# More banks for spare matmuls, and VectorE work moved between groups, in a fused two-attention kernel

## Chip, cores and metric

The kernel runs on one NeuronCore of a Trainium2 chip. The metric is the device time of one execution in microseconds (us), as a median of separate runs. TensorE does the matmuls (PE in the profile, its weight loads are PEld), ScalarE (ACT) does the exponentials, VectorE (DVE) the elementwise work, SyncE (SP) issues most transfers.

## What is computed

Two attention layers read the same input of 2,048 rows and 640 columns, with 32 heads of 20 columns each. Layer A is full softmax attention; layer B looks at eight earlier positions, two apart. A gate per row mixes the two.

```
def _A_ref(x, wqkv, wo):
    ...
    scores = jnp.einsum("bhqd,bhkd->bhqk", q, k) * scale
    p = _softmax(scores, axis=-1)
    o = jnp.einsum("bhqk,bhkd->bhqd", p, v)
    return (...)(o, 0, 2, 1, 3).reshape(B, S, D) @ wo
...
def _B_ref(x, wqkv, wo):
    W, dil = 8, 2
    ...
    logits = jnp.einsum("bhsd,bhswd->bhsw", q, kg) * scale
    logits = jnp.where(mask[None, None, :, :], logits, -1e9)
    attn = _softmax(logits, axis=-1)
    o = jnp.einsum("bhsw,bhswd->bhsd", attn, vg)
    return (...)(o, 0, 2, 1, 3).reshape(B, S, D) @ wo
...
g = _sigmoid((x * gate_w).sum(-1, keepdims=True))
return g * a + (1 - g) * b
```

## The kernel before

**Groups and units.** Layer A is worked in 32 groups: four chunks of 512 queries, and in each chunk eight quads of four heads. A group has 64 units, one for each of 16 key blocks and four heads. A unit is the score matmul of 128 keys against 512 queries (L1172, it fills one PSUM bank), an exponential and a value matmul (L1196). PSUM has eight banks. Banks 0 to 2 and 3 to 4 take the scores in turn: a step of the kernel is one exponential of ScalarE over three banks, the next over two (`mk_exp`, L1187). The value matmuls of a group add up in bank 5 (`OB`), each head in its own strip of 32 partitions. At the end of a group VectorE transposes bank 5 out (`do_norm`, L644), and only then can the next group's values start there.

**Units on VectorE.** `XN` gives for each of the 32 groups how many of its units are not exponentiated on ScalarE. `gen_x` (L985 to L1020) does such a unit: a score matmul (L995) into a side bank, seven VectorE operations that make the exponential by a polynomial (L1000 to L1008), and a value matmul into bank 5 (L1017). The tuple adds up to 36 units, which leaves 2,012 units and 805 steps for ScalarE.

**Lanes.** Banks 6 and 7 are side banks. All other work is written as generators, called lanes, that take a side bank, fill it by matmuls, let VectorE copy it out, and give it back: `gen_k`, `gen_q` and `gen_v` make layer A's keys, queries and values; `gen_F` projects layer B's queries and keys and its logits (L827, L843); `gen_K` projects layer B's values, does its softmax (L900 is its exponential on ScalarE) and the weighted sum over eight positions on VectorE (L957, L961); `gen_fold` applies the output weights and sends the result out (L694); `gen_prefold` does so for the last chunk up to its last two quads. `FWIN`, `KWIN` and `OWIN` give, for each chunk, the groups between which the lanes F, K and O (fold) are paced: before the first number the lane isn't due, by the second it should be done, and from the step before that on it is due at every step. A lane also waits for what it depends on, for example K of chunk 1 for K of chunk 0.

**The planner.** The order of every engine's instructions is made when the program is built. A loop over the 805 steps (L1351) books costs on a clock for each engine (`clk`), issues the score matmuls two steps ahead, holds values back until three steps are pending or bank 5 is free (`flush`, L1408), then lets due lanes issue what fits before TensorE's and VectorE's limits for this step (`lim_pe`, `lim_dve`). `take` (L438) marks a side bank as held and `give` (L455) frees it, with the time at which its last copy ends in `free_at`. Waits follow from what tasks read and write (`task`, L82). A task that *writes* a buffer waits for the last writer and for all readers, also when the last writer is on its own engine. A task that *accumulates* waits for readers, but not for an earlier writer on its own engine.

**Spare matmuls.** After the lanes, the loop at L1492 adds matmuls whose result nobody reads. It aims at so much side work on TensorE for each step that is pending:

```
while pair_side < FILL * min(3, npend) and clk["pe"] + MM + SWITCH <= lim_pe and s < NS - 2 and npv[0] == 0:
    if not idle_mm():
        break
```

`FILL` is two matmuls of 512 columns, `MM` is booked as 0.216 us. `idle_mm` (L1303) writes a side bank that no lane holds (L1315, identity times a piece of the input). If there is none, it accumulates zeros onto bank 5 (L1319), if that bank is neither read nor still to be read by VectorE. Otherwise it does nothing. Where spares are still missing after an even step, the next score matmuls are issued twice or three times (`dup`).

Of the kernel before, what the change touches and what calls it, by code (L numbers as in the profile page):

```python
# [13 lines left out]
P = 128  # L14
# [4 lines left out]
CN = D // P  # L19
# [13 lines left out]
XMIN = -126.0 / (SCALE * 1.4426950408889634)  # L33
XLOG = float(np.log(2.0 / XC4))

XN = (1, 2, 0, 2, 0, 2, 1, 2, 0, 0, 0, 0, 0, 1, 2, 1, 1, 0, 0, 3, 0, 2, 1, 1, 2, 2, 3, 1, 1, 1, 2, 2)
FWIN = ((3.5, 2.1), (8.7, 7.6), (13.9, 21.4), (20.8, 24.3))
KWIN = ((7.6, 8.5), (9.5, 12.4), (12.6, 24.7), (24.0, 23.4))
OWIN = ((6.1, 13.1), (13.7, 23.5), (15.7, 31.2))
XPOS = ((7, 1), (9, 2), (5, 0), (11, 3))  # L40


# [203 lines left out]
def _build(ctx, nc, A_x, A_wqkv, A_wo, B_wqkv, B_wo, gate_w, out):  # L246
# [83 lines left out]
    def fap(t, first, dims):  # L330
        return bass.AP(tensor=t, offset=first.offset, ap=[[first.ap[0][0], P]] + dims)
# [97 lines left out]

    held = {6: False, 7: False}  # L430
    free_at = {6: 0.0, 7: 0.0}
    forcing = [0]
    cur = [None]
    EAGER = "kqvx"
# [3 lines left out]
    def take():  # L438
        while True:
            free = [b for b in (6, 7) if not held[b]]  # L440
            me = cur[0].name if cur[0] is not None else ""
            hot = me[:1] in EAGER
            if hot:
                wanting.add(me)
            if free and (hot and (me[0] != "v" or not any(w[0] != "v" for w in wanting)) or not wanting or forcing[0]):
                b = min(free, key=lambda k: free_at[k])
                if forcing[0] or free_at[b] <= clk["pe"] + 100.0:
                    held[b] = True
                    wanting.discard(me)
                    if cur[0] is not None:  # L450
                        cur[0].hold += 1
                    return b
            yield ("poll",)
# [12 lines left out]
    def chain(b, mms, reads, w=1.0, cost=MM):  # L466
        n = len(mms)
        for k, m in enumerate(mms):
            yield ("pe", cost, w)
            t = mm_part(b, [m], k, n, reads, cost)  # L470
        return t

# [4 lines left out]
    def v_chunk(b, p, gi, kb, i_):  # L477
        lo, hi = VG[gi]
        w0, wn = (1, 161) if p == 0 else (2 + 160 * p, 160)

        def fn(e):
            ins = None
            for c in range(CN):
                ins = e.matmul(bank[b][:, i_ * wn:(i_ + 1) * wn], xT[:, c, kb * P:(kb + 1) * P],  # L484
                               WvA[:, c, w0:w0 + wn], start=(c == 0), stop=(c == CN - 1))
            return ins

        rd = ["xT"] + (["WvA0", "WvA1"] if p == 0 else ["WvA"])
        if i_ == 0:
            return T("pe", fn, reads=rd, writes=[("bk", b)], cost=375)  # L490
        return T("pe", fn, reads=rd, accum=[("bk", b)], cost=375)
# [303 lines left out]
    def gen_F(tc):  # L795

        while not latedone[0] or (tc > 0 and not fdone.get(tc - 1)):
            yield ("poll",)
        xk = [("x_tm", t) for t in range(NCH)] if tc == 0 else []
        if tc == 0:  # L800
            T("dve", lambda e: e.memset(kB[:, :, 0:PADB], 0.0), writes=["kB"] + xk, cost=100)
        else:
            T("dve", lambda e: e.tensor_copy(kB[:, :, 0:PADB], kB[:, :, 512:512 + PADB]), reads=["kB"], writes=["kB"], cost=170)
        for kind in ("q", "k"):
            for f in range(CN):
                b = yield from take()
                w0 = f * P if kind == "q" else D + f * P
                mms = [(bank[b], WqkB[:, c, w0:w0 + P], xT[:, c, tc * 512:(tc + 1) * 512]) for c in range(CN)]
                t = yield from chain(b, mms, ["WqkB", "xT"])
                dst, key = (qB[:, f, :], "qB") if kind == "q" else (kB[:, f, PADB:PADB + 512], "kB")  # L810
                yield ("dw", t.fin, 690.0, 0.0)
                give(b, T("dve", lambda e, dst=dst, b=b: e.tensor_copy(dst, bank[b]), reads=[("bk", b)], writes=[key], cost=690))  # L812
        while tc > 0 and not ldone.get(tc - 1):
            yield ("poll",)
        while (NQUAD - 1) not in wk_made:
            yield ("poll",)
        for half in range(2):
            b = yield from take()
            slot = {}

            def sel(f, b=b, slot=slot):
                rs = [slot[(f, wp)] for wp in range(4)]

                def pe_l(e):
                    ins = None
                    for wp in range(4):
                        ins = e.matmul(bank[b][32 * wp:32 * wp + 32, :], Sel[:, f, :], prod[rs[wp]][:, :],  # L827
                                       start=(f == 0), stop=(f == CN - 1))
                    return ins

                rd = [("prod", r) for r in rs] + ["Sel"]
                if f == 0:
                    return T("pe", pe_l, reads=rd, writes=[("bk", b)], cost=340)
                return T("pe", pe_l, reads=rd, accum=[("bk", b)], cost=340)

            for idx in range(4 * CN):
                f, wp = divmod(idx, 4)
                r = prodctr[0] % NPR
                prodctr[0] += 1
                slot[(f, wp)] = r  # L840
                off = PADB - DIL * (4 * half + wp)
                yield ("dve", 416.0, 0.2)
                t = T("dve", lambda e, r=r, f=f, off=off: e.tensor_tensor(prod[r][:, :], qB[:, f, :], kB[:, f, off:off + 512],  # L843
                                                                      ALU.mult),
                      reads=["qB", "kB"], writes=[("prod", r)], cost=416)
                if idx >= 5 and idx % 4 == 1:
                    yield ("pe", 340.0, 0.0)
                    sel(idx // 4 - 1)
            yield after(t)
            yield ("pe", 340.0, 0.0)  # L850
            t = sel(CN - 1)
            yield ("dw", t.fin, 690.0, 0.0)
            give(b, T("dve", lambda e, half=half, b=b: e.tensor_copy(lgt[half], bank[b]),
                      reads=[("bk", b)], writes=[("lgt", half), ("WkA", 1)], cost=690))
        if tc == 0:
            for w in range(1, WIN):
                row = 32 * (w % 4)
                T("dve", lambda e, w=w, row=row: e.memset(lgt[w // 4][row:row + 32, 0:DIL * w], -1.0e9),
                  writes=[("lgt", w // 4)], cost=60)
        fdone[tc] = True  # L860

    def gen_K(tc):
# [25 lines left out]
            return ins  # L888

        yield ("pe", 550.0, 300.0)  # L890
        t = T("pe", pe_tf, reads=[("lgt", 0), ("lgt", 1), "ident"], writes=[("bk", b)], cost=550)
        yield ("dw", t.fin, 690.0, 690.0)
        give(b, T("dve", lambda e, b=b: e.tensor_copy(L_flat, bank_bf[b]), reads=[("bk", b)], writes=["L"], cost=690))
# [43 lines left out]
        yield after(mk_rep(0))  # L937
        b = yield from take()
        yield ("pe", 550.0, 300.0)
        t = mk_aT(0, b)  # L940
        yield ("dw", t.fin, 690.0, 690.0)
        give(b, ev_aT(0, b))
        for bl in range(4):
            ai = bl % 2
            for w in range(WIN):
# [23 lines left out]
                if w == 3 and bl < 3:  # L969
                    yield after(tr)  # L970
                    b = yield from take()
                    yield ("pe", 550.0, 300.0)
                    tm = mk_aT(bl + 1, b)
                if w == 4 and bl < 3:
                    yield ("dw", tm.fin, 690.0, 690.0)
# [9 lines left out]
    def gen_x(gi, k, u):  # L985
# [3 lines left out]
        while gi > 0 and not (gi in ql and ql[gi].done):  # L989
# [2 lines left out]
        kA, kB_, kC = "xA", "xB", "xC"  # L992
        b = yield from take()
        yield ("pe", MM, 0.0)
        t = T("pe", lambda e: e.matmul(bank[b], kT[32 * j:32 * j + 32, q, kb * P:(kb + 1) * P], qT[gi % NQT][32 * j:32 * j + 32, :],  # L995
                                       start=True, stop=True),
              reads=[("kT", q, kb // 4), ("qT", gi % NQT)], writes=[("bk", b)], cost=MM)
# [304 lines left out]

    def idle_mm():  # L1303

        free = [b for b in (6, 7) if not held[b] and free_at[b] <= clk["pe"] + 50.0]
        obs = [sch.bufs[("ob", j)] for j in range(4)]
        if not free and (any(o[1] for o in obs) or any(o[0].stream != "pe" for o in obs)):
            return False
        sw = 0.0 if block[0] else SWITCH
        clk["pe"] += sw  # L1310
        block[0] = True
        block[1] += MM
        if free:
            b = free[0]
            T("pe", lambda e: e.matmul(bank[b], ident[:, :], xT[:, 0, 0:512], start=True, stop=True),  # L1315
              reads=["xT", "ident"], writes=[("bk", b)], cost=MM)
        else:

            T("pe", lambda e: e.matmul(bank[OB], zt[:, :], fap(ident, ident[:, 0:1], [[0, 4], [1, P]]), start=False, stop=False,  # L1319
                                       skip_group_check=True),  # L1320
              reads=["zt", "ident"], accum=[("ob", j) for j in range(4)], cost=MM)
        return True

    kl, vl, ql, foldl, xl = {}, {}, {}, {}, {}
# [221 lines left out]
```

## Time and profile before

| | |
|---|---|
| three timed runs | 950.94, 953.43, 954.73 us; median 953.43 |
| the profiled execution, its own time | 949.74 us |
| its span, first to last instruction | 947.9 us |
| mean granted TensorE clock | 0.995 |
| ScalarE busy | 927.7 us, 831 instructions |
| VectorE busy | 702.7 us, 1,305 instructions |
| TensorE busy by its modelled ends | 846.1 us, 6,241 matmuls |
| exponentials of three banks (402) and two (403) | 1,579 and 1,152 ns each |
| spare matmuls, by weight loads | 251 of L1315, 31 of L1319 |

A row of the profile that begins with a line number is a group of like instructions: line, engine, operation, output and inputs, count, busy time in us and mean of one in ns, and the idle time before them with what ended it. An exponential's own time is longer than the distance to the next one, since ScalarE starts an instruction before the last has left it; the distance between starts is what counts. A stretch is a piece of the span with each engine's busy time in it and the TensorE clock that was granted, 1.00 at full speed.

### The profile page before, as it was taken

What the parts mean: (1) busy time and instruction counts of PE and PEld (TensorE: products, weight loads), DVE (VectorE), ACT (ScalarE), POOL (GpSimd) and SP (SyncE); (2) the same over time, 40 slices, a digit from 0 to 9 for tenths busy, and PEclk for the clock granted to TensorE, in tenths of its full rate; (3) what the DMA queues carried; (4) which work ended last, traced back from release to release, by engine and by line L of the source; (5) the groups of instructions that cost most, each with busy time, mean ns of one, the idle gap of its engine ahead of it and who ended that gap; (6) DMA issues with size and microseconds to landing.
All of it is one profiled execution on the core that took longest, in us unless ns stands there. A gap on an engine that the chain in (4) does not pass through costs nothing.

```text
span 947.9 us, 16453 instructions
## 1 busy us (share of the span) xinstructions
PE 846.1 (89%) x6241; PEld 284.9 (30%) x6337; DVE 702.7 (74%) x1305; ACT 927.7 (98%) x831; POOL 3.1 (0%) x7
## 2 busy tenths in 40 slices
PE   8989899988888888999888899888888999889897
PEld 5333233322222222333222223322222233322232
DVE  5687664756777888548989775788898867898853
ACT  5999999999999999999999999999999999999997
POOL 1000000000000000000000000000000000000000
PEclk9999999999999999999999999999999999999999
DMA  9000000000000000000000000000000000000000
GB/s 312 9 1 4 22 13 1 1 22 16 1 1 2 1 1 1 8 8 8 8 1 1 1 1 8 8 9 1 8 2 1 1 8 8 15 1 1 1 1 28
DMA packets 12033, 12.86 MB, mean 14 GB/s; under 512 B 3380, under 2 KB 11316, under 8 KB 11956
## 3 DMA queue, kind: packets, MB, share of 16 engines
q1 hardware_dynamic: 9844, 11.43, 3.7%
q8 instruction: 52, 0.85, 0.4%
q10 hardware_dynamic: 2112, 0.37, 0.2%
q14 instruction: 25, 0.20, 0.1%
HBM read 9.18 MB, written 2.62 MB: 12 GB/s over the span
## 4 chain that ended last, share of the span: by engine, by line
ACT 70%; issue 16%; PE 12%; DVE 1%; DMA 1%; SPq 0%; ACTq 0%; DVEq 0%
ACT ebuf L1187 69%; PE ps L1172 4%; PE ps L401 2%; PE ps L1315 2%; PE ps L1196 2%; DMA x_tm<-in_A_x_dram 1%; PE ps L484 0%; ACT L_sb L900 0%; PE ps L1039 0%; DVE mx L896 0%; DVE Kmax L1070 0%; PE ps L1017 0%; DVE L_sb L898 0%; PE ps L995 0%; PE ps L887 0%
## 5 line engine op out<-in xcount | busy, mean ns | idle before, releaser
L1187 ACT ACTIVATE ebuf<-ps 128x1536 bf16<-128x1536 f32 (+1 forms) x805 | 913.4, 1365 | 4.5 <-PE ps L1172 3.4
L1172 PE MATMUL ps<-qT,kT 32*128 32x512 bf16 x2050 | 320.9, 384 | 75.7 <-ACT ebuf L1187 64.2
L1172 PEld LDWEIGHTS ps<-qT,kT 32*128 32x128 bf16 x2050 | 88.3, 91 | 344.5 <-issue 153.3
L1196 PE MATMUL ps<-ebuf,vA 128*21 128x512 bf16 x2012 | 171.9, 384 | 0.0
L1315 PE MATMUL ps<-xT,ident 128*128 128x512 bf16 x220 | 85.4, 389 | 10.7 <-PE ps L1172 5.0
L957 DVE TENSOR_TENSOR bw<-vB,bw 128x640 f32<-128x640 bf16 x112 | 91.8, 820 | 1.9
L961 DVE TENSOR_TENSOR blkacc<-blkacc,bw 128x640 f32<-128x640 f32 x96 | 78.8, 821 | 1.9
L843 DVE TENSOR_TENSOR prod<-qk 128x512 bf16<-128x512 bf16 x160 | 58.7, 419 | 18.8 <-PE ps L827 18.6
L1196 PEld LDWEIGHTS ps<-ebuf,vA 128*21 128x21 bf16 x2012 | 42.2, 90 | 73.8 <-issue 51.1
L644 DVE STREAM_TRANSPOSE rg<-ps 128x512 f32<-128x512 f32 x31 | 22.2, 717 | 52.7 <-PE ps L1196 52.7
L401 PE MATMUL ps<-xT,WqkB 128*128 128x512 bf16 x179 | 55.4, 383 | 1.6 <-issue 1.6
L401 PE MATMUL ps<-woA_r,oTn 128*128 128x320 bf16 x240 | 50.3, 303 | 0.2 <-PE ps L1172 0.2
L1315 PEld LDWEIGHTS ps<-xT,ident 128*128 128x128 bf16 x251 | 24.0, 96 | 68.7 <-PE ps L1315 39.8
L401 PE MATMUL ps<-xT,WqP 128*128 128x512 bf16 (+1 forms) x152 | 43.2, 378 | 1.6 <-issue 1.0
L1000 DVE TENSOR_SCALAR xb<-ps 128x512 int32<-128x512 f32 x36 | 24.8, 688 | 25.5 <-PE ps L995 14.9
L401 PE MATMUL ps<-xT,WkP 128*128 128x512 bf16 (+1 forms) x144 | 40.6, 379 | 2.2 <-PE ps L1172 0.8
L580 DVE CAST qT<-ps 128x512 bf16<-128x512 f32 x31 | 21.4, 690 | 24.7 <-PE ps L401 24.7
L413 DVE TENSOR_SCALAR kT<-ps,e 128x512 bf16<-128x512 f32 x28 | 20.9, 746 | 20.8 <-PE ps L401 17.9
L401 PE MATMUL ps<-WvA,oBacc 128*128 128x320 bf16 x160 | 34.3, 307 | 1.4 <-issue 0.8
L875 DVE CAST vB<-ps 128x512 bf16<-128x512 f32 x20 | 13.8, 690 | 26.3 <-PE ps L401 26.1
L812 DVE CAST qk<-ps 128x512 bf16<-128x512 f32 x40 | 27.4, 684 | 8.0 <-PE ps L401 7.6
L401 PE MATMUL ps<-xT,WvB 128*128 128x512 bf16 x90 | 32.7, 384 | 0.2 <-issue 0.2
(120 smaller groups left out, 676.5 us busy)
## 6 DMA issues: line engine op xcount, KB each, us to landing
x_tm<-in_A_x_dram SPq DMA_DIRECT2D x3, 640.0 KB
out_dram<-outsb SPq DMA_DIRECT2D x12, 160.0 KB
WqkB<-in_B_wqkv_dram SPq DMA_DIRECT2D x1, 1600.0 KB
WqkA<-in_A_wqkv_dram SPq DMA_DIRECT2D x2, 700.0 KB
qk<-in_B_wqkv_dram SPq DMA_DIRECT2D x1, 800.0 KB
woA_r<-in_A_wo_dram SPq DMA_DIRECT2D x32, 25.0 KB
WvA<-in_B_wo_dram SPq DMA_DIRECT2D x5, 160.0 KB
x_tm<-in_A_x_dram SPq DMA_DIRECT2D x2, 320.0 KB
```

Of the source, the lines that this page charges most:

```text
L401: ins = e.matmul(o, l, r, start=(k0 + k == 0), stop=(k0 + k == n - 1))
L580: T("dve", lambda e: e.tensor_copy(qt[:, :], bank[b]), reads=[("bk", b)], writes=[("qT", gi % NQT)], cost=690)
L644: return T("dve", lambda e: e.transpose(rg[i][:, :], bank[OB]), reads=[("ob", j) for j in range(4)], writes=["rg"], cost=720)
L812: give(b, T("dve", lambda e, dst=dst, b=b: e.tensor_copy(dst, bank[b]), reads=[("bk", b)], writes=[key], cost=690))
L843: t = T("dve", lambda e, r=r, f=f, off=off: e.tensor_tensor(prod[r][:, :], qB[:, f, :], kB[:, f, off:off + 512], ALU.mult), reads=["qB", " ...
L957: T("dve", lambda e, vv=vv, av=av: e.tensor_tensor(tmpB, vv, av, ALU.mult), reads=[("aT", ai), "vB4"], writes=["tmpB"], cost=822)
L961: T("dve", lambda e: e.tensor_tensor(blkacc[:, :, :], blkacc[:, :, :], tmpB, ALU.add), reads=["tmpB"], writes=["blkacc"], cost=822)
L1000: give(b, T("dve", lambda e: e.tensor_scalar(Ai, bank[b], float(XMIN), float(XMUL), op0=ALU.max, op1=ALU.mult), reads=[("bk", b)], writes= ...
L1172: ins = e.matmul(bank[b0 + i], kT[32 * j:32 * j + 32, q, kb * P:(kb + 1) * P], qT[gi % NQT][32 * j:32 * j + 32, :], start=True, stop=True)
L1187: return T("act", lambda e: e.activation(ebuf[s % NEB][:, 0:512 * n], ps[:, b0 * 512:(b0 + n) * 512], ACTF.Exp, bias=XLOG, scale=SCALE), r ...
L1196: ins = e.matmul(bank[OB][32 * j:32 * j + DH + 1, :], vA[:, q, kb, VW * j:VW * j + DH + 1], ebuf[s % NEB][:, i * 512:(i + 1) * 512], start ...
L1315: T("pe", lambda e: e.matmul(bank[b], ident[:, :], xT[:, 0, 0:512], start=True, stop=True), reads=["xT", "ident"], writes=[("bk", b)], cos ...
```

## The change

Three tuples of windows and the tuple of units are new, with the same sum of 36 units. A record `state` tells for each held side bank whether it was just taken and not yet written ("new"), is in the middle of an accumulating chain of 512-column matmuls ("sum"), or neither. `idle_mm` gets two more places: a side bank that is held but still new is treated like a free one; bank 5 may be overwritten when VectorE has read it out and nothing new is in it (`rest`); and zeros may be accumulated onto a side bank in the middle of a chain, which goes before the zeros onto bank 5.

```
-XN = (1, 2, 0, 2, 0, 2, 1, 2, 0, 0, 0, 0, 0, 1, 2, 1, 1, 0, 0, 3, 0, 2, 1, 1, 2, 2, 3, 1, 1, 1, 2, 2)
-FWIN = ((3.5, 2.1), (8.7, 7.6), (13.9, 21.4), (20.8, 24.3))
-KWIN = ((7.6, 8.5), (9.5, 12.4), (12.6, 24.7), (24.0, 23.4))
-OWIN = ((6.1, 13.1), (13.7, 23.5), (15.7, 31.2))
+XN = (1, 2, 0, 2, 1, 0, 2, 1, 0, 1, 0, 0, 0, 0, 3, 2, 0, 0, 0, 3, 0, 1, 2, 1, 2, 2, 3, 1, 0, 2, 1, 3)
+FWIN = ((3.8, 2.6), (8.7, 6.2), (13.9, 21.4), (21.1, 23.5))
+KWIN = ((7.6, 9.0), (5.5, 11.3), (10.4, 25.2), (25.3, 26.7))
+OWIN = ((2.4, 12.1), (13.4, 23.8), (14.6, 31.6))
...
+    state = {6: "", 7: ""}
...
                     held[b] = True
+                    state[b] = "new"
...
             t = mm_part(b, [m], k, n, reads, cost)
+            state[b] = "sum" if k < n - 1 and cost == MM else ""
...
                 rd = [("prod", r) for r in rs] + ["Sel"]
+                state[b] = "sum" if f < CN - 1 else ""
...
     def idle_mm():
 
-        free = [b for b in (6, 7) if not held[b] and free_at[b] <= clk["pe"] + 50.0]
         obs = [sch.bufs[("ob", j)] for j in range(4)]
-        if not free and (any(o[1] for o in obs) or any(o[0].stream != "pe" for o in obs)):
+        now = clk["pe"] + 50.0
+        free = [b for b in (6, 7) if (not held[b] or state[b] == "new") and free_at[b] <= now]
+        sums = [b for b in (6, 7) if held[b] and state[b] == "sum"]
+        rest = all(o[1] for o in obs) and max(t.fin + 56.0 for o in obs for t in o[1]) <= now
+        if not (free or sums or rest) and (any(o[1] for o in obs) or any(o[0].stream != "pe" for o in obs)):
             return False
...
+        zeros = fap(ident, ident[:, 0:1], [[0, 4], [1, P]])
         if free:
             b = free[0]
             T("pe", lambda e: e.matmul(bank[b], ident[:, :], xT[:, 0, 0:512], start=True, stop=True),
               reads=["xT", "ident"], writes=[("bk", b)], cost=MM)
+        elif rest:
+
+            T("pe", lambda e: e.matmul(bank[OB], ident[:, :], xT[:, 0, 0:512], start=True, stop=True),
+              reads=["xT", "ident"], writes=[("ob", j) for j in range(4)], cost=MM)
         else:
 
-            T("pe", lambda e: e.matmul(bank[OB], zt[:, :], fap(ident, ident[:, 0:1], [[0, 4], [1, P]]), start=False, stop=False,
-                                       skip_group_check=True),
-              reads=["zt", "ident"], accum=[("ob", j) for j in range(4)], cost=MM)
+            b = sums[0] if sums else OB
+            T("pe", lambda e: e.matmul(bank[b], zt[:, :], zeros, start=False, stop=False, skip_group_check=True),
+              reads=["zt", "ident"], accum=[("bk", b)] if sums else [("ob", j) for j in range(4)], cost=MM)
         return True
```

At the other places where a lane writes a side bank whole (values, transposes of layer B, a VectorE unit's scores) `state` is set back to neither.

## Prediction

> **What bounds the kernel now.** I read the page's busy shares first, then its costliest groups, then single stretches.
>
> ```profile
> PE 846.1 (89%) x6241; PEld 284.9 (30%) x6337; DVE 702.7 (74%) x1305; ACT 927.7 (98%) x831; POOL 3.1 (0%) x7
> ...
> ACT 70%; issue 16%; PE 12%; DVE 1%; DMA 1%; SPq 0%; ACTq 0%; DVEq 0%
> ...
> L1187 ACT ACTIVATE ebuf<-ps 128x1536 bf16<-128x1536 f32 (+1 forms) x805 | 913.4, 1365 | 4.5 <-PE ps L1172 3.4
> ```
>
> ScalarE is busy for 98% of the span, and 805 exponentials make nearly all of it. The change keeps 36 VectorE units, so it keeps 2,012 units and 805 exponentials. Only the distance between exponentials can change.
>
> In the trace's start times, the first exponential begins at 19.2 us and the last ends at 940.0; 7.9 us of closing work follow. The shortest distance from one start to the next is 1.330 us after a three-bank exponential and 0.904 us after a two-bank one: 402 pairs at 2.234 us would take 898.1 us. They take 919.5 (402 times the mean distances, 1.360 and 0.927). The **21.5 us too many** split as follows, by adding up each step's excess:
> - 4.84 us in three places where TensorE's granted clock is halved (below): 1.47 us near 108, 1.51 us near 440, 1.85 us near 487.
> - 3.81 us at the four softmax exponentials of the local branch (L900), 0.95 us each. They stay, wherever they are moved.
> - 3.82 us after groups of three spare matmuls (below).
> - 2.47 us in twelve other steps of over 0.1 us, and 6.5 us of steps under 0.1 us.
>
> The halved clock is seen by cutting the span into stretches of 3.413 us that start where the first halving starts. The columns are stretch, length, busy time of PE, PEld, DVE, ACT and POOL (with instructions), granted clock, DMA.
>
> ```profile
> 104.86:108.27 3.41, 2.42 (x19) 0.74 (x18) 1.68 (x3) 3.41 (x4) 0.00 (x0) 1.00 0.08 23
> 108.27:111.68 3.41, 3.41 (x17) 0.65 (x13) 3.14 (x9) 2.89 (x3) 0.00 (x0) 0.50 0.07 17
> 275.52:278.94 3.42, 1.95 (x12) 0.75 (x13) 2.26 (x2) 3.42 (x4) 0.00 (x0) 1.00 0.00 0
> 435.95:439.36 3.41, 1.76 (x22) 0.55 (x19) 3.06 (x7) 3.41 (x5) 0.00 (x0) 1.00 0.00 0
> 439.36:442.77 3.41, 3.41 (x17) 1.06 (x13) 3.20 (x4) 2.56 (x3) 0.00 (x0) 0.50 0.00 0
> 483.74:487.15 3.41, 2.03 (x12) 0.64 (x14) 3.38 (x8) 3.41 (x4) 0.00 (x0) 1.00 0.03 5
> 487.15:490.56 3.41, 3.41 (x19) 0.69 (x20) 2.64 (x5) 1.97 (x3) 0.00 (x0) 0.50 0.00 0
> 712.43:715.84 3.41, 2.31 (x18) 0.84 (x19) 2.01 (x6) 3.41 (x5) 0.00 (x0) 1.00 0.00 0
> ```
>
> Each halved stretch (0.50) follows one in which PE was thinly used. Of some 270 stretches of this grid these are among the seven thinnest, but the order is not strict: 275.52 with 1.95 us busy and 712.43 with 2.31 are not followed by a halving, 104.86 with 2.42 is. In a halved stretch PE is busy throughout and ACT falls to 1.97 to 2.89 us: ScalarE waits for scores.
>
> **Thin stretches lie where spares could not run.** At 483.74 one side bank collects a projection (L401), the other waits for its copy (L934), and the values' bank is being read by the norm transpose (L644, at 482.9): until the next values at 487.99 the spare code runs late and little. L644 starts at 77.3, 106.6, 249.1, 307.7, 482.9, 512.8, 598.9, 629.4 and 714.4 us, inside or within 2.3 us of nine of the fifteen thinnest stretches. So group starts are thin. The stretch at 435.95 is another case: it holds a local-branch exponential (L900 at 435.2), which keeps the score banks 1.1 us longer while PE waits.
>
> **The change part by part.**
>
> *Spares in more places.* A spare matmul is one 512-column matmul. Its price on the path is in its neighbours:
>
> ```profile
> 686.36 1.29 PE L1315 MATMUL ps<-xT,ident 128*128 128x512 bf16 x3
> 687.58 0.39 PE L1172 MATMUL ps<-qT,kT 32*128 32x512 bf16 x3
> 687.90 1.29 PE L1315 MATMUL ps<-xT,ident 128*128 128x512 bf16 x3
> 689.13 0.39 PE L1172 MATMUL ps<-qT,kT 32*128 32x512 bf16 x2
> ...
> PEld ps L1315 <- PE ps L1315: 39.8, 122, 0.4
> ```
>
> Spares of L1315 start 0.450 us apart, because each writes the bank that the last one wrote and waits for it (the wait row: 122 times, 39.8 us). The planner books 0.216 plus 0.100. The accumulating spares of L1319 have no such wait and start 0.226 us apart. By weight loads (31 matmul records of L1315 are missing) L1315 runs alone 41 times, in twos 81 times and in threes 14 times, without counting runs mixed with L1319. After a single or a two the next exponential is on time: median excess 0.010 and 0.001 us, over 0.1 us only 8 times in 122. After a three it is late **14 times out of 14**, by 0.14 to 0.49 us on one to three steps (0.82 and 1.04 in the halved stretch at 487). The thirteen outside it cost 3.82 us, 0.29 us each. Twelve of the fourteen come within 4 us after an L644: there values are held back, three steps are pending, and the loop's target is highest.
>
> So each place that the change opens may get one or two spares free, or a three for 0.29 us. I take seven new threes, one for each of the six thin group starts that have none now (77, 106, 249, 513, 599 and 629) and one more at 483: 7 x 0.29 = **+2.1 us**. The bounds: nothing, if they come as twos or as zero matmuls; or two threes at each of those, 14 x 0.29 = +4.1.
>
> A spare in a held, still unwritten bank makes the lane's first matmul wait for it: 0.450 less 0.226, about 0.22 us on TensorE, which is hidden as after today's twos. A spare in the values' bank delays the group's first values in the same way, 0.22 us, in front of L1196, whose results are wanted only at the group's end. Both at nothing; uncovered, 31 group starts x 0.22 = 6.8 us, which I keep in the high end.
>
> *Halved stretches.* Group starts at 106.6 and 482.9 get filled: 1.47 + 1.85 = **-3.3 us**. The one at 435.95 is not short of banks, and moving the local branch moves it without removing the L900; I leave its 1.51 in. Bounds: -4.84 (all go) and +3.0 (two more appear where units now lie, such as 275.52).
>
> *The 36 units.* By L1000 to L1008 a unit is 0.688 + 0.422 + 0.681 + 0.416 + 0.682 + 0.683 + 0.683 = 4.26 us of DVE. Fifteen groups change their number, each by one except group 5 (two fewer). DVE has 702.7 of 947.9 us, but locally less room: group 15 (450.8 to 479.5) has 26.30 us busy of 28.70 and gets one more, 30.6. The overflow of 1.9 us is taken from the paced local products (L957, ten there), which slide into the next group, relieved of a unit. The last group goes from two to three: 12.86 + 4.26 = 17.1 of 28.7. Nothing, then; without that cover a unit forced at a group's end holds TensorE for up to its 4.26 us. Low end nothing, high end one such hold.
>
> *Windows of the local branch.* The same instructions and DMAs are issued; output DMAs (L694, twelve of 160 KB) move on SP's queue with the folds, where only the weight loads of the start stand before them. K1 already waits for K0 to end, K3 starts up to 1.3 groups (37 us) later, and its last products and the prefold have DVE slack in groups 30 and 31 (19.54 and 12.86 us busy of 28.7). Nothing, with the same 4.26 us as the bound.
>
> **The sum.** Profiled execution: 949.74 us (947.9 and 1.8 around). 949.74 - 3.3 + 2.1 = 948.5. The three timed runs have a median of 953.43, which is 3.7 above, and spread over 3.8 us. At 1.6 us a halving that is about two halved stretches more than the profiled run had; this is an inference, since those runs have no trace. If two thirds of these go as well, as in the sum above, 3.7 becomes 1.2 to 1.5: 948.5 + 1.5 = **950.0 us**.
>
> The row first: the second halving starts 331.1 us after the first and the third 47.8 us after that, 97 and 14 times 3.413, so they lie on one grid. [...]
>
> **Rivals.**
> - *Fewer halvings than I think* (0.25). The moves by occupancy lift every thin stretch, the one with the L900 too, and the new spares come as twos or zero matmuls: 949.74 - 4.84 = 944.9, and about 1.5 for the timed runs gives 946. For: seven thin stretches hold the risk, and most are group starts. Against: the 14 threes show that the loop makes threes just there.
> - *The lows only move* (0.18). A unit taken from one group thins another, and as many halvings remain: 953.4. For: 1.95 us busy escaped and 2.42 did not, so a small shift decides.
> - *Spares close nothing* (0.05): what halves the clock is not this thinness, and new threes are pure cost: 953.43 + 2.1 = 955.5. [...]
> - *Slower, by threes* (0.10): the values' bank, rest at every group start, draws a three there. From 12 new ones (12 x 0.29 = 3.5) the gain is eaten; at two more for each of 18 group starts, 36 x 0.29 = 10.4, less 3.3 for the halvings and half the 3.7 us, gives 958.7. For: 14 of 14 threes are late. Against: 81 twos are not.
>
> **How the numbers follow.** The forecast has 0.42, its own range is 947 to 953. The range to 8 in 10 reaches from 945.5 (most of the first rival) to 956.5 (rivals two and three, and the low part of the fourth). About 0.5%, 4.8 us, is what a measurement here can tell from no change: faster means under 948.7, slower over 958.2. Faster: 0.23 of the first rival and 0.10 of the forecast's lower part, 0.33. Slower: 0.08 of the last rival and 0.01 of the others, 0.09. The rest, 0.58, is within.
>
> **What would show it.** Stretches with a granted clock of 0.50: at most one in the profile after, none at a group start. Spares between an L644 and the next values, writing the values' bank. Runs of three spares: about 21, each followed by a late exponential. L1187 unchanged at 805, and L900 still costing 0.95 us each. I am wrong if halvings remain after stretches that were filled, if threes no longer delay scores, or if time is lost at a group's end to a VectorE unit (PE waiting for L1008's output).

## The result, and the profile after

The kernel after takes 947.29 us (median of six runs, 945.64 to 948.90), the kernel before 951.5 us in the six runs beside them (950.78 to 954.73). The ratio is 0.9949, with a 95% interval of 0.9930 to 0.9967. The forecast was 950.0, its range 945.5 to 956.5.

The page of the kernel after, in the lines that answer to those shown before:

```profile
span 945.9 us, 16569 instructions
...
PE 870.7 (92%) x6350; PEld 285.2 (30%) x6350; DVE 704.3 (74%) x1305; ACT 927.3 (98%) x831; POOL 3.1 (0%) x7
...
ACT 70%; issue 16%; PE 12%; DVE 1%; DMA 1%; SPq 0%; ACTq 0%; DVEq 0%
...
L1197 ACT ACTIVATE ebuf<-ps 128x1536 bf16<-128x1536 f32 (+1 forms) x805 | 913.1, 1366 | 2.8 <-PE ps L1182 1.8
```

ScalarE does the same 805 exponentials (now L1197). The profiled execution took 947.71 us, 2.0 less than before, and that is what the distances between exponentials lost: 917.5 us where they were 919.5. Split as in the prediction: the halved clock 2.47 us (it was 4.84), four local-branch exponentials 3.82 (3.81), late steps behind threes 4.05 (3.82).

The stretches of 3.413 us, cut on this execution's own grid:

```profile
104.45:107.86 3.41, 2.32 (x17) 0.61 (x15) 1.28 (x3) 3.41 (x5) 0.00 (x0) 1.00 0.11 26
107.86:111.27 3.41, 3.38 (x17) 0.77 (x18) 3.36 (x10) 2.56 (x3) 0.00 (x0) 0.50 0.07 19
111.27:114.69 3.42, 3.42 (x11) 0.64 (x9) 1.05 (x3) 2.46 (x3) 0.00 (x0) 0.50 0.09 22
...
425.30:428.71 3.41, 2.49 (x19) 0.72 (x17) 2.46 (x6) 3.41 (x4) 0.00 (x0) 1.00 0.00 0
```

Before, seven stretches had under 2.43 us of TensorE busy; now one has, and it is the one that a halving follows (two grid stretches long). The next thinnest has 2.49. This doesn't hang on where the grid lies: over 24 positions of it there are on average 6.4 such stretches before and 0.7 after, 4.4 with the new places alone and 2.7 with the new units alone. The halvings near 440 and 487 are gone; the one near 108 stayed.

**Every run tells its halvings.** Each run has a mean granted clock. Each of the three halvings in the profile before is 3.413 us at 0.50, which takes 0.5 x 3.413 us from about 950, 0.0018 of the mean; so (1 - clock) / 0.0018 counts them (in the two kernels of about 1,000 us, the count goes by their own span; a stretch that the end of the span cuts off counts in part). From here on a halving is one such stretch. Over 68 runs of the kernel before the mean is 4.4 halvings, from 2 (948.54 us) to 10 (958.63 us). Over six runs of the kernel after it is 1.4: 0, 1, 1, 1, 2 and 3. A straight line through a kernel's runs, time against halvings, rises by 1.04 to 1.49 us for each halving in the kernels of the table that have few, and gives a time at no halving. Three fewer halvings at 1.2 us are 3.6 of the 4.2 us between the medians; the rest is within what six runs can tell.

| kernel | median us | ratio to before (95%) | halvings a run | line at none, us |
|---|---|---|---|---|
| before | 951.4 | 1 | 4.4 | 946.5 |
| after | 947.3 | 0.9949 (0.9930 to 0.9967) | 1.4 | 945.8 |
| new places alone | 947.4 | 0.9955 (0.9938 to 0.9973) | 2.3 | 945.4 |
| units alone | 949.1 | 0.9962 (0.9944 to 0.9980) | 1.8 | 946.0 |
| units and windows alone | 953.7 | 1.0016 (0.9999 to 1.0033) | 2.0 | 951.1 |
| after, spares don't wait | 945.4 | 0.9917 (0.9895 to 0.9939) | 1.3 | 943.6 |
| after, third left out | 945.0 | 0.9917 (0.9897 to 0.9937) | 1.1 | 943.5 |
| third left out, old windows | 944.8 | 0.9929 (0.9915 to 0.9943) | 1.0 | 943.5 |
| third left out, repeats to bank 5 | 944.7 | 0.9929 (0.9914 to 0.9945) | 1.5 | 943.0 |
| new places alone, no wait | 948.1 | 0.9955 (0.9933 to 0.9977) | 3.2 | 943.5 |
| after, spares in pairs | 954.7 | 1.0022 (1.0005 to 1.0040) | 1.3 | 952.6 |
| after, zero weights | 947.9 | 0.9956 (0.9942 to 0.9970) | 1.3 | 945.7 |
| after, no spares or repeats | 994.6 | 1.0438 (1.0399 to 1.0477) | 81 | |
| after, spares on 32 rows | 1011.2 | 1.0631 (1.0610 to 1.0652) | 71 | |

### The profile page after: what moved, and what is told of

The parts are those of the page before. It is cut to its first block, busy times and chain, and to the rows that moved or that the text cites. A ratio compares the mean times of both kernels' runs of the same rounds, so it can differ in the third digit from the quotient of the medians.

```text
span 945.9 us, 16569 instructions
## 1 busy us (share of the span) xinstructions
PE 870.7 (92%) x6350; PEld 285.2 (30%) x6350; DVE 704.3 (74%) x1305; ACT 927.3 (98%) x831; POOL 3.1 (0%) x7
## 4 chain that ended last, share of the span: by engine, by line
ACT 70%; issue 16%; PE 12%; DVE 1%; DMA 1%; SPq 0%; ACTq 0%; DVEq 0%
ACT ebuf L1197 69%; PE ps L1182 4%; PE ps L401 3%; PE ps L1329 2%; PE ps L1206 2%; DMA x_tm<-in_A_x_dram 1%; PE ps L488 0%; ACT L_sb L907 0%; PE ps L1049 0%; PE ps L832 0%; DVE mx L903 0%; DVE Kmax L1080 0%; PE ps L1027 0%; DVE L_sb L905 0%; PE ps L1005 0%
## 5 line engine op out<-in xcount | busy, mean ns | idle before, releaser
L1197 ACT ACTIVATE ebuf<-ps 128x1536 bf16<-128x1536 f32 (+1 forms) x805 | 913.1, 1366 | 2.8 <-PE ps L1182 1.8
L1329 PE MATMUL ps<-xT,ident 128*128 128x512 bf16 x291 | 113.0, 389 | 7.4
L401 PE MATMUL ps<-xT,WqkB 128*128 128x512 bf16 x200 | 61.5, 384 | 0.0
L1329 PEld LDWEIGHTS ps<-xT,ident 128*128 128x128 bf16 x291 | 27.9, 96 | 77.9 <-PE ps L1329 51.5
L401 PE MATMUL ps<-woA_r,oTn 128*128 128x320 bf16 x240 | 50.0, 301 | 0.0
L401 PE MATMUL ps<-xT,WkP 128*128 128x512 bf16 (+1 forms) x165 | 46.4, 383 | 0.0
L401 PE MATMUL ps<-xT,WqP 128*128 128x512 bf16 (+1 forms) x165 | 46.2, 376 | 0.2
L585 DVE CAST qT<-ps 128x512 bf16<-128x512 f32 x31 | 21.4, 690 | 22.4 <-PE ps L401 22.2
L401 PE MATMUL ps<-xT,WvB 128*128 128x512 bf16 x100 | 34.5, 384 | 0.0
L401 PE MATMUL ps<-WvA,oBacc 128*128 128x320 bf16 x160 | 33.3, 301 | 0.4 <-PE ps L1182 0.4
L602 DVE CAST qT<-ps 128x512 bf16<-128x512 f32 x31 | 21.4, 690 | 13.3 <-PE ps L595 13.1
```

What stands on the lines that cost most here:

```text
L401: ins = e.matmul(o, l, r, start=(k0 + k == 0), stop=(k0 + k == n - 1))
L585: T("dve", lambda e: e.tensor_copy(qt[:, :], bank[b]), reads=[("bk", b)], writes=[("qT", gi % NQT)], cost=690)
L602: return T("dve", lambda e: e.tensor_copy(qT[gi % NQT][:, :], bank[b]), reads=[("bk", b)], writes=[("qT", gi % NQT)], cost=690)
L1197: return T("act", lambda e: e.activation(ebuf[s % NEB][:, 0:512 * n], ps[:, b0 * 512:(b0 + n) * 512], ACTF.Exp, bias=XLOG, scale=SCALE), r ...
```

## The experiments

The theory: the gain is fewer halvings, because group starts were filled. The rivals: that the moved units did it, that spares close nothing, that the gain is somewhere else.

**The places alone.** The kernel after with the four old tuples.

```
-XN = (1, 2, 0, 2, 1, 0, 2, 1, 0, 1, 0, 0, 0, 0, 3, 2, 0, 0, 0, 3, 0, 1, 2, 1, 2, 2, 3, 1, 0, 2, 1, 3)
+XN = (1, 2, 0, 2, 0, 2, 1, 2, 0, 0, 0, 0, 0, 1, 2, 1, 1, 0, 0, 3, 0, 2, 1, 1, 2, 2, 3, 1, 1, 1, 2, 2)
...
-KWIN = ((7.6, 9.0), (5.5, 11.3), (10.4, 25.2), (25.3, 26.7))
+KWIN = ((7.6, 8.5), (9.5, 12.4), (12.6, 24.7), (24.0, 23.4))
...
```

> The new places for spares with the old tuples of units and windows. The theory that the gain is fewer halved stretches because spares now reach the thin group starts: about 947.5 us, mean clock 0.997 or more, most stretches under 2.4 us of PE busy gone. The rival, that the moved units and windows thicken the thin stretches and the new places do little (the profile after shows only 3 spares in the values' bank and 21 zero matmuls): about 951 us, clock 0.995 as before.

Measured 947.42 us at 2.3 halvings. The places alone bring it to the time of the whole change, though not to its clock: five stretches are under 2.43 us of TensorE busy, where before seven were, and the halvings lie between before (4.4) and after (1.4). What the places do is small: weight load by weight load, the order differs from before at seven group starts (79, 250, 307, 396, 482, 541 and 598 us), in two zero spares that become spares in a side bank, and in one projection matmul that moves by a step near 490 us. There are 297 spares for 282, and 22 fewer repeated scores (2,028 score matmuls for 2,050). At 482, the kernel before:

```profile
483.26 0.39 PE L1172 MATMUL ps<-qT,kT 32*128 32x512 bf16 x3 [0.42 <-ACT ebuf L1187]
483.59 0.39 PE L401 MATMUL ps<-xT,WqkB 128*128 128x512 bf16 x1
484.18 0.61 PE L1172 MATMUL ps<-qT,kT 32*128 32x512 bf16 x4 [0.20 <-ACT ebuf L1187]
485.52 0.39 PE L1172 MATMUL ps<-qT,kT 32*128 32x512 bf16 x3 [0.74 <-ACT ebuf L1187]
```

and with the new places, at the same step:

```profile
481.78 0.39 PE L1182 MATMUL ps<-qT,kT 32*128 32x512 bf16 x3 [0.42 <-ACT ebuf L1197]
482.11 0.39 PE L401 MATMUL ps<-xT,WqkB 128*128 128x512 bf16 x1
482.33 0.38 PE L1333 MATMUL ps<-xT,ident 128*128 128x512 bf16 x1
482.64 0.39 PE L1182 MATMUL ps<-qT,kT 32*128 32x512 bf16 x2
482.96 0.60 PE L1338 MATMUL ps<-ident,zt 128*128 128x512 bf16 x2
484.04 0.39 PE L1182 MATMUL ps<-qT,kT 32*128 32x512 bf16 x3 [0.47 <-ACT ebuf L1197]
```

Before, two score matmuls are issued twice (x4) and TensorE then idles 0.74 us. With the places, one spare goes to the values' bank (L1333) and two zero matmuls to an accumulator (L1338), the scores are issued once, and no clock is halved here.

**The tuples alone.** The kernel before with the four new tuples (the same lines as above, the other way round, in the old code).

> The new tuples with the old places for spares. If the new places made the gain: about 951 us, clock about 0.995. If the tuples made it: about 947.5 us, clock 0.997 or more. In this order the prefold is not done five steps before the end and is forced there, which both theories let cost something at the end of the span (0 to 4 us, seen as idle ScalarE in the last 20 us and not elsewhere).

Measured 953.74 us, though its halvings fell to 2.0. The loss is one wait on ScalarE, before its last two exponentials:

```profile
924.37 15.03 ACT L1187 ACTIVATE ebuf<-ps 128x1536 bf16<-128x1536 f32 x13
943.37 1.94 ACT L1187 ACTIVATE ebuf<-ps 128x1024 bf16<-128x1024 f32 x2 [3.97 <-PE ps L1172]
```

In these 4 us TensorE does the last pieces of the prefold (L401 at 938.30 to 939.79), VectorE copies them (L714, L715 to 941.8), and only then come the closing matmuls and the next scores. In this order the prefold was late; in the kernel after, and with the units alone, it isn't.

**The units alone.** The kernel before with the new `XN` line and nothing else.

> The new units of VectorE alone: old windows, old places for spares. The tuples together brought the halvings of a run from 4.4 to 2.0 but lost 4.3 us at one step near the end, where the prefold was forced. In this order the prefold is done in time. If the units are what thickens the thin stretches: about 2 to 2.5 halvings, clock 0.996, about 948 us. If it was the windows: clock 0.992 as before, about 951 us.

Measured 949.11 us at 1.8 halvings. The units by themselves thicken the thin stretches: three under 2.43 us of TensorE busy for seven, and 313 spares fit for 282, all in the old places. So both halves of the change do the same thing, and together they give less than the sum of the two: 3.0 halvings fewer, not 2.1 + 2.6.

**No spares.** The kernel after with `FILL = 0.0` for `FILL = 2.0 * MM`.

> The kernel after without any spare matmul and without repeated scores (the target of side work is zero). If halved stretches are what the spares are for, and each costs 1.04 to 1.23 us as the runs so far show: many more of them, clock 0.985 or less (8 or more stretches), 955 us or more. The rival (spares close nothing, threes are pure cost): no more halvings than now, no late steps behind threes, about 943 us.

Measured 994.58 us, about 81 halvings. Spares and repeated scores are taken out together here; the rival that they close nothing is refuted.

**Threes.** In the kernel after there are sixteen threes for fourteen, and fourteen of them are late. Two forms take their waits away in the same order of instructions. The first lists a spare as accumulating, so it doesn't wait for the spare before it:

```
-              reads=["xT", "ident"], writes=[("bk", b)], cost=MM)
+              reads=["xT", "ident"], accum=[("bk", b)], cost=MM)
...
-              reads=["xT", "ident"], writes=[("ob", j) for j in range(4)], cost=MM)
+              reads=["xT", "ident"], accum=[("ob", j) for j in range(4)], cost=MM)
```

> The kernel after, in the same order on every engine, but a spare matmul does not wait for the matmul before it in its bank (it stands as an accumulation in the list of dependences). The theory that runs of three are late because each spare waits 0.450 us for the last: spares start 0.226 us apart, none of the 18 late steps behind threes is left, 4.0 us less: about 943.3 us. The rival, that three spares are too many whatever their distance: 947.3 us as the kernel after. A second one: packed closer, the same spares leave TensorE idle longer at a stretch and the clock is halved more often: over 945 us at a clock under 0.996.

The second leaves the third spare of a step out and books its time all the same:

```
+        got = 0
...
+            if got == 2:
+                clk["pe"] += MM + 100.0
+                block[1] += MM
-            if not idle_mm():
+            elif not idle_mm():
                 break
+            got = min(2, got + 1)
```

> The kernel after, in the same order, with the third spare of a run left out (its time is still booked): 16 spares fewer. The theory of the waits: 4.0 us less, about 943.3 us, if the thirds are not needed against the halving. If they are needed, halved stretches come back behind group starts, 1.1 to 1.8 us each: 945 to 949 us with a clock under 0.996.

Measured 945.36 and 945.01 us, at 1.3 and 1.1 halvings. The same step, first in the kernel after and then without the wait:

```profile
685.27 0.39 PE L1182 MATMUL ps<-qT,kT 32*128 32x512 bf16 x3
685.60 1.29 PE L1329 MATMUL ps<-xT,ident 128*128 128x512 bf16 x3
686.82 0.39 PE L1182 MATMUL ps<-qT,kT 32*128 32x512 bf16 x2
```

```profile
686.32 0.39 PE L1182 MATMUL ps<-qT,kT 32*128 32x512 bf16 x3 [0.20 <-ACT ebuf L1197]
686.64 0.82 PE L1329 MATMUL ps<-xT,ident 128*128 128x512 bf16 x3
687.39 0.39 PE L1182 MATMUL ps<-qT,kT 32*128 32x512 bf16 x2
```

From scores to scores it is 1.55 us with the waits and 1.07 without. At their shortest distance two exponentials take 2.234 us, so a step has 1.117 on average: the first is late and the second isn't. But only half came: the line at none fell by 2.2 us, not by 4.0. Step by step against the kernel after, 4.0 us went from 19 late steps, and 2.4 us came back in 320 other steps, each longer by 0.001 to 0.020 us. What lengthens those isn't shown.

The same wait taken away with the old tuples:

> The new places with the old tuples, and spares that do not wait for the spare before them. By terms: the new places with old tuples measured 947.4 us at 2.3 halvings; without the waits of threes 2.0 us less, as between the kernel after and its form without waits: 945.4 us at about 2.3 halvings. If packing spares closer brings more halvings here, where more thin stretches are left: up to 947.4.

Measured 948.07 us. The line at none fell as expected (945.4 to 943.5), but the halvings rose from 2.3 to 3.2, which eats it. With the new tuples they did not rise. Twelve and eleven runs don't settle whether closer packing causes more of them.

**More spares in the same time.** Spares don't wait, the first two of a step are two matmuls each, the third is left out:

```
+            def two(e):
+                for _ in range(2):
+                    ins = e.matmul(bank[b], ident[:, :], xT[:, 0, 0:512], start=True, stop=True)
+                return ins
...
+            T("pe", two, reads=["xT", "ident"], accum=[("bk", b)], cost=MM)
```

> The kernel after with twice the spares in side banks at the same TensorE time: a spare does not wait for the one before it, the first two of a step are issued as two matmuls each (0.226 us apart), the third is left out. If thickness of work is what counts against the halving, fewer than the 1.1 to 1.4 halvings of the kernel after and of its other two forms: clock 0.998 or more, and 943.5 to 944.5 us. If the remaining halvings lie where no spare runs at all (near 105 us, seen in every profile with the new tuples): the same 1.1 to 1.4, about 945 us. If the extra matmuls delay scores: late steps come back, over 946 us.

Measured 954.66 us, slower than before, at 1.3 halvings:

```profile
557.42 0.39 PE L1182 MATMUL ps<-qT,kT 32*128 32x512 bf16 x2
557.74 1.04 PE L1331 MATMUL ps<-xT,ident 128*128 128x512 bf16 x4
558.71 0.39 PE L1182 MATMUL ps<-qT,kT 32*128 32x512 bf16 x3
```

Four back to back make 1.29 us from scores to scores, 0.17 more than a step has. One such step is often still on time; where fours stand in successive steps, as at 556, 558 and 559 us here, the exponentials fall behind (0.33 us at 558). 72 steps are late by over 0.1 us, for 20 in the form with the third left out. So a wait isn't needed to be late: scores, spares and the next scores have to fit into 1.117 us on average.

**Windows.** The form with the third left out, with the old `FWIN`, `KWIN` and `OWIN`.

> The kernel after with the third spare of a run left out and the old windows of the lanes F, K and O: new places and new units only. The form with the new windows measured 945.0 us at 1.1 halvings. If the windows matter in the final kernel: 2 or more halvings, 946.5 us or more. If they do not (units alone had 1.8 halvings, units and windows 2.0): 945 us at about 1.1.

Measured 944.83 us at 1.0 halvings: beside the places and the units, the windows do nothing that can be seen.

**What counts against a halving.** The kernel after with all spares of L1329 and L1333 on 32 rows, in the same places and order (L1333 is changed in the same way):

```
-            T("pe", lambda e: e.matmul(bank[b], ident[:, :], xT[:, 0, 0:512], start=True, stop=True),
+            T("pe", lambda e: e.matmul(bank[b], ident[0:32, :], xT[0:32, 0, 0:512], start=True, stop=True),
...
```

> The kernel after with the same spares at the same times in the same banks, but each on 32 of the 128 rows of TensorE. If the halving goes by the time in which any matmul streams: 947.3 us at 1.4 halvings, as the kernel after. If it goes by rows at work: a spare is worth a quarter, and the halvings come near to those without any spare (78, at 994.6 us): at least 20 of them, over 965 us.

Measured 1011.24 us, about 71 halvings, nearly as many as without spares (81; the 78 above counts them by a span of 950 us). Its page, and a stretch with the halved one behind it:

```profile
PE 917.6 (91%) x6277; PEld 280.4 (28%) x6350; DVE 704.9 (70%) x1305; ACT 938.4 (93%) x831; POOL 3.1 (0%) x7
...
PEclk9999999999999566998987779999856699866699
```

```profile
322.97:326.39 3.42, 3.00 (x22) 1.00 (x22) 2.56 (x6) 3.42 (x4) 0.00 (x0) 1.00 0.00 0
326.39:329.80 3.41, 3.31 (x23) 0.61 (x21) 3.24 (x8) 3.15 (x3) 0.00 (x0) 0.50 0.00 0
```

TensorE looks as busy as before (91% of the span; 90% outside the halved stretches, where the kernel after has 92%), and the clock (tenths, 40 slices) is halved in 17 places. One thing besides the rows changes: a spare on 32 rows starts earlier, 0.22 us behind the scores for 0.32 (medians), which could leave TensorE idle for longer. That isn't the cause: with spares on 32 rows, the 17 stretches before the clock falls have TensorE busy for 2.6 to 3.1 us with no idle time over 0.4 us; in the other thirteen profiles all 35 such stretches, without the start and the closing work, have 2.42 or less.

Then with weights of zero (`zt`) in place of the identity:

> The kernel after with the same spares at the same times, but with weights of zero in place of the identity. If the halving goes by time of streaming: 947.3 us at 1.4 halvings. If matmuls with zeros count less (the zero spares on bank 5 and on chains would then be of little use): many more halvings, over 960 us.

Measured 947.87 us at 1.3 halvings, the same as with the identity. So here a spare on 32 rows did not replace one on 128 (71 halvings for 1.4), and weights of zero did as well as the identity (1.3 for 1.4). Rows, and cells of the array (rows times columns), can't be told apart here, since every spare kept its 128 columns.

**Repeated scores.** Scores are matmuls of 32 rows. In the form with the third left out, six of the seven places where scores are repeated get spares in bank 5 behind the scores instead (`mk_qk(s + 2, 0)`, then as many matmuls like that of L1333).

> The kernel after with the third spare of a run left out, and where scores would be issued twice or three times while the values' bank has been read out, that many spares go to the values' bank behind the scores instead (six places of seven). Scores use 32 rows a matmul, spares 128. If a spare is thicker than repeated scores: under 1.1 halvings and about 944.3 us, above all none at 105 to 115 us. If both count the same by their time: 945.0 us at 1.1. If the spares hold back the next values: late ends of groups, over 945.5.

Measured 944.65 us at 1.5 halvings, beside 945.01 at 1.1: no difference that six runs can show. A halving near 108 us is still in its profile, but none of the six places (166, 339, 483, 655, 712 and 797 us) lies near it.

## Why the prediction was right, and where it was off

The direction and the mechanism held: thin stretches were filled, and halvings went. The places held only in part, and half of the means, the moved units, had been put at nothing. Step by step:

- *Halvings, -3.3 us in the profiled execution.* Measured -2.4, and not the two that I named: of 108 and 487 only 487 went, while 440, which I left in, went as well. With the new units the local exponential is at 425 us, where the stretch (2.49 us busy, the second thinnest) was not followed by a halving; with the places alone it is still at 434, and a halving follows at 438. One profile doesn't tell which place is cured. Near 108 us the kernel after is halved and its form with zero weights isn't, in the same order; with the places alone it isn't either, though nothing near 106 us differs from before. In these two profiles the grid (its place is explained in the last section) begins at 1.46 and 1.04 us; the ten other profiles with spares on 128 rows are all halved near 108 us, and in nine of them it begins between 2.05 and 3.21. It is the counts over all runs that show the gain.
- *Seven new threes, +2.1 us.* This is the term that was mis-sized. There are two more in all, and late steps behind threes cost 4.05 us for 3.82: +0.2. The price of 0.29 us each was right, the number wasn't: of the seven places named, one got a three (627.7 us), and it isn't late. With the places alone, three of the seven changed group starts got a three, the others singles, twos and zero matmuls, and two old threes went.
- *Where the spares go.* I expected the values' bank. It took three of 315 (L1333), and 21 were zero matmuls (L1338); the other 291 are in side banks.
- *The units, nothing.* They cost nothing on VectorE, as said, but they are worth 2.6 halvings alone. I looked at what they take from VectorE and not at what they leave for TensorE.
- *The windows, nothing with a bound of 4.26 us.* Nothing in the kernel after. With the old places the late prefold cost 3.97 us at the end, near the bound, but by TensorE's and VectorE's work on the prefold and not by a unit.
- *From the profiled run to the median, 3.7 us.* Too much: it rested on three runs. In 68 runs the median is 951.4, which is 1.6 above the profiled one. That the gap is made of halvings was an inference; the granted clock of every run now shows it.
- *Rivals.* "Spares close nothing" is refuted by the run without spares (81 halvings). "Slower by threes" did not come, since the threes did not. The first rival, few halvings and 946, was nearer than the forecast in time and in its ground: one stretch under 2.43 us was left of seven, the one with the local exponential was lifted too, and the new spares came mostly as singles and twos. It was wrong in that a halving is left, 2.47 us of it in the profile.

Two sizes were off to opposite sides: I counted 5.5 us for halvings with the runs' offset (4.8 in the profile and 3.7 above it, of which 3.0 were to stay), and they gave 3.6; I charged 2.1 for threes, and they took 0.2. That the forecast change (-3.4 us from a median of three runs that lay high) came near the measured one (-4.2) is in part luck.

## What to carry to other kernels

Where spare matmuls keep TensorE's clock (here 81 halvings without them and the repeated scores, 1.4 with), look for the few thinnest stretches and fill those; fifteen more spares at seven places, in place of repeated 32-row scores, were worth 4 us, while twice the spares everywhere cost 9.7 us against the form with the third left out (954.7 and 945.0). Let a spare use all rows: on 32 of the 128 the same spares were worth almost nothing here (71 halvings). Before adding one, add up the time from one needed matmul to the next, with the waits that the spare itself makes: here about 1.1 us was free, and 1.29 in successive steps was late. Every run's granted clock tells more than its time: with it, runs that differ by 5 us lie on one line.

## What the runs showed of the hardware

A busy TensorE did not keep its clock by itself in these runs; how much of the array the spares used counted too: 294 spares on 32 rows instead of 128 let the halvings rise from 1.4 to 71, with TensorE busy for 91% of the span. Spares with zero weights counted as well as those with the identity (1.3 halvings against 1.4).

Halved stretches came in lengths of 3.413 us and its multiples (but where the span ends): 3.413 three times in the profile before, twice that in the one after (6.83, from 107.86 to 114.69), three times that with the units alone (10.24, from 108.89 to 119.13). In each profile with several of them they fit one grid: with the places alone they begin at 437.95 and 608.62, 50 steps of 3.413 apart. Its place against the first instruction differs between profiles: carried back by steps of 3.413 us, it begins at 2.46 us in the profile before, at 2.05 in the one after, at 3.07 with the units alone and at 1.04 with the places alone. The longest idle time of TensorE in a stretch before a halving was 1.46 us in the profile before (up to 437.44 us), and 0.4 us with spares on 32 rows.
